# Three products in place of four for the 32 rest channels of a spectral layer

## The chip, the cores and the metric

The kernel runs on one core of a Trainium2 chip. Its time is the device time of one execution in microseconds, the median of several runs. The engines named below are TensorE (PE; its weight loads are PEld), VectorE (DVE), ScalarE (ACT), GpSimd (POOL) and SyncE (SP), which issues most of the DMA transfers.

## The reference

```python
# x: [2, 1, 4096, 640]; w1, w2: [2 (re, im), 4 blocks, 160, 160]; b1, b2: [2, 4, 160]
Xf = rfft2(x, axes=(1, 2))                    # 2049 frequencies
zr, zi = real and imaginary part of Xf.reshape(B, H, Wf, 4, 160)
hr = relu(einsum(zr, w1[0]) - einsum(zi, w1[1]) + b1[0])
hi = relu(einsum(zi, w1[0]) + einsum(zr, w1[1]) + b1[1])
or_ = einsum(hr, w2[0]) - einsum(hi, w2[1]) + b2[0]
oi_ = einsum(hi, w2[0]) + einsum(hr, w2[1]) + b2[1]
a = irfft2(softshrink(or_) + 1j * softshrink(oi_))      # threshold 0.01
b = (gelu(x @ w_gate) * (x @ w_up)) @ w_down            # 640 -> 1728 -> 640
g = sigmoid((x * gate_w).sum(-1))
out = g * a + (1 - g) * b
```

All is fp32, and the kernel reaches that accuracy by splitting operands into a high and a low part (`split`: ScalarE makes the high part in L290, VectorE the low part in L293), so one real product costs three matmuls.

## The kernel before

Three stages follow each other. In the first (0 to about 1315 us) TensorE works on the gate and up projections of the feed-forward part, with the forward Fourier transform's first pass and the preparation of the spectral weights among it. The second is the spectral stage (about 1317 to 1715 us). The third is the down projection with the second pass of the inverse transform.

The change lies in the second. The frequencies are cut into 16 chunks of 256 (one, chunk (0,0), has 258 and is called wide). Each chunk takes four *steps*, one for each block `n` of 160 channels; `steps` lists all 64, and one Python loop over `i` writes the instructions of step `i`, so that order of emission is the order on each engine. For each `i` it writes, in this order: the events of the step (loads; `rest` for the next chunk in the step of block 1), `main_z` of step `i + 1`, `mlp1` of step `i` (layer 1), `mlp2` of step `i - 1` (layer 2), and after every second step the first pass of the inverse transform, `inv1`. Each engine executes its own list in order and waits at semaphores for the others.

A block's 160 channels don't fit 128 partitions. `main_z` transforms the first 128 of them: four L1001 products into one PSUM bank, whose content is split into `z` (high and low; 512 columns hold real and imaginary part). It also makes their sum: ScalarE copies the imaginary part (`zt`, L1013), VectorE adds the real part (L1016), and a split gives `zs`. That split is not written at once: `fwd2` returns it as a function, which `mlp1` calls as `sums()` behind its VectorE additions L1111. The 32 *rest* channels of all four blocks, 128 together, are transformed once per chunk by `rest`, which writes their split `zz` to DRAM (`zld`) so that `zl_load` can bring them back block by block with other partitions.

Layer 1 uses three real products for the 128 main channels: `pk` with the weights times `zs`, and a `group` for each of `hr` and `hi` with `z`, to which `pk` is added (ScalarE copies `pk` to `kc` in L1104, VectorE adds in L1111, then ScalarE and VectorE make `h` in L1064 and L1065). The rest channels enter the two groups by four real products, in two matmuls for each group: `zl1` has 128 rows, `zl2` 66 rows with two rows of ones for the bias. `last` (L1087 to L1089) gives the 32 rest *outputs* into bank `pl`; its last reader is VectorE's L1118, which adds the bias `b1r`. PSUM has eight banks, handed out in turn by `bank()`: a product that takes a bank waits for the last reader of the bank's former content.

The calls that the edit replaces are these:

```python
def rest(b, c):
    z = zmid(b, c, [P, 2, 2, width(b, c)], F32R, name="zz")
    fwd2(b, c, 4 * P, [z[:, h] for h in range(2)])
    ...
at(4 * ch - 3 - lead[1], 1, rest, b, c)
at(4 * ch - 2 - lead[2], 1, zl_load, b, c)
```

Of the kernel before, what the change touches and what calls it, by code (L numbers as in the profile page):

```python
# [43 lines left out]
def _tables():  # L44
# [97 lines left out]
    sgn = np.zeros((P, 4))  # L142
# [3 lines left out]
    sgn[:, 3] = 1 - (p // 2) % 2  # L146
# [21 lines left out]
def _layouts(a):  # L168

    A = lambda n: np.asarray(a[n])  # L170
    c = np.ascontiguousarray
# [41 lines left out]
    def long1(w):
        m, r = w[..., :P], w[..., P:]
        return np.concatenate([m[0], m[1], r[0], r[1]], axis=-1)
# [19 lines left out]
def spectral_mix_kernel(ctx: ExitStack, tc: tile.TileContext, a):  # L235
# [39 lines left out]
    zld = [[dram.tile([P, 4 * CW], F32, name=f"zl_{b}{c}") for c in range(NCH)] for b in range(2)]  # L275
# [580 lines left out]
    def prep(l, pb):  # L856
# [5 lines left out]
        def loads():  # L862
            o["m"] = [small([P, 480], name="raw") for q in range(2)]
            for q in range(2):
                ld(o["m"][q], a[nm + "m"][:, ns[q]])
# [4 lines left out]
        def wide_high(q):  # L870
            m = o["m"][q]
            if l == 1:
# [5 lines left out]
                high(w[:, P:384], m[:, 224:])  # L878
# [5 lines left out]
        def wide_low(q):  # L884
# [4 lines left out]
            if l == 1:  # L889
# [4 lines left out]
                low(w[:, LOW1 + P:], m[:, 224:], w[:, P:384])  # L894
# [4 lines left out]
        def st1():  # L899
            rl, rs = o["l"], o["s"]  # L900
            for m in o["m"] if l == 1 else ():
                nc.vector.tensor_add(m[:, :P], m[:, :P], m[:, 224:352])
                nc.vector.tensor_sub(m[:, 352:], m[:, 352:], m[:, 224:352])
            sg = sgn[:, l - 1:l]
            for cs in ((slice(0, BS),) if l == 2 else (slice(0, P), slice(256, 288))):
                nc.vector.tensor_scalar(rl[:, :, cs], rl[:, :, cs], sg, None, op0=OP.mult)
                nc.vector.tensor_scalar(rs[:64, :, cs], rs[:64, :, cs], sg[:64], None, op0=OP.mult)
            if l == 2:
                nc.vector.tensor_scalar(rs[64:66], rs[64:66], LAM, None, op0=OP.add)
# [6 lines left out]
        def st3():  # L916
            wide_low(1)
            t = o["t"] = big([P, 2, 2, 320], F32R, name="wl")
# [3 lines left out]
            nc.gpsimd.memset(t[64:, :, 1, 0 if l == 2 else 64:].bitcast(F32), 0.0)  # L922
# [3 lines left out]
        def st4():  # L926
            t, bf = o["t"], o["b"].bitcast(F32)
            hi, lo = (t[:, :, 0], t[:, :, 1]) if l == 2 else (t[:, :, 0], t[:, :, 1, 64:])
            n = 320 if l == 2 else 256
            nc.vector.tensor_sub(lo[:64], o["s"][:64, :, :n], bf[:64, :, :n])  # L930
            nc.vector.scalar_tensor_tensor(lo[64:66], bf[64:66, :, :n], sgn[64:66, 2:3], o["s"][64:66, :, :n],
                                           op0=OP.mult, op1=OP.add)
# [22 lines left out]
    zl2, hl1, hl2, HW, WT = [], [], [], {}, []  # L955
# [9 lines left out]
    def ones():  # L965
        zl2.append(mid([P, NBLK, CH], F32R, name="zl2"))
        nc.gpsimd.memset(zl2[-1][64:].bitcast(F32), 0.0)
        nc.gpsimd.memset(zl2[-1][64:66].bitcast(F32), 1.0)

# [57 lines left out]
    def rest(b, c):  # L1027

        z = zmid(b, c, [P, 2, 2, width(b, c)], F32R, name="zz")
        fwd2(b, c, 4 * P, [z[:, h] for h in range(2)])  # L1030
        d = zld[b][c]
        if wide(b, c):
            st(d, z.rearrange("p h r f -> p (h r f)").bitcast(F32))
        else:
            st(dr(d, 0, [[4 * CW, P], [CW, 4], [1, CH]]), z[:, :, :, :CH].rearrange("p h r f -> p (h r) f").bitcast(F32))

    def zl_load(b, c):
        F = width(b, c)
# [5 lines left out]
        ld(t[:, :, :F].bitcast(F32), dr(d, 0, [[CW, P], [P * CW, NBLK], [1, F]]))
        for n in range(NBLK):
            ld(t2[:64, n, :F].bitcast(F32), dr(d, n * P * CW, [[4 * CW, 32], [CW, 2], [1, F]]))
# [20 lines left out]
    def mlp1(b, c, n, sums):  # L1067
# [15 lines left out]
        def last(dst):
# [5 lines left out]
            nc.tensor.matmul(dst, wl[:, 256:384], by_two(t1[:, n, :F]), start=False, stop=True, skip_group_check=True)  # L1089
# [12 lines left out]
        mms(pk[:, :F], [(wh, sh[:, :F]), (wh, sl[:, :F]), (wlo, sh[:, :F])])  # L1102
# [682 lines left out]
```

## Time and profile before

| | |
|---|---|
| median of three runs | 2408.78 us (2407.82 to 2409.89) |
| the profiled execution | 2407.91 us |
| its span in the trace | 2406.1 us |
| spectral stage | about 1317 to 1715 us |
| one chunk of four steps in its middle | 24.7 us |
| TensorE clock granted | 1.00 throughout |

The page gives busy time of each engine, the chain of work that ended last, and groups of equal instructions. The waits view adds up, for one engine, how long an instruction had to wait and which instruction ended the wait; its columns are the total, the number of times and the longest. The timeline lists instructions with start, duration, engine, source line, output and inputs, and in brackets the idle time before them with what ended it. The windows view gives the engines' busy time in stretches of the span.

### The profile page before, as it was taken

Reading aid. Unit: us, or ns where it says so; the run is one execution under the profiler, and the core shown is the slowest. Engines: PE = TensorE matmul, PEld = TensorE weight load, DVE = VectorE, ACT = ScalarE, POOL = GpSimd, SP = SyncE. Lnnn points to the kernel's source line nnn. Section 1 sums busy time; section 2 is a strip of 40 time slices with the busy share of each in tenths; the row PEclk is TensorE's granted clock in tenths of the full one; section 3 lists DMA queues with packets and bytes.
Section 4 is the critical chain, followed back from the end, with each engine's and each line's share of the span. In section 5 each row is a group of like instructions: output and inputs, shape, how many; then the busy total and the mean of one; then the engine's idle time right before and its main releaser. Section 6 shows DMA issues by size and latency. Waiting matters only on the chain.

```text
span 2406.1 us, 49143 instructions
## 1 busy us (share of the span) xinstructions
PE 2397.7 (100%) x18047; PEld 2391.9 (99%) x18047; DVE 1969.7 (82%) x4150; ACT 1464.5 (61%) x3332; POOL 143.0 (6%) x213
## 2 busy tenths in 40 slices
PE   9999999999999999999999999999999999999999
PEld 9999999999999999999999999999999999999999
DVE  8777779777778888888857888888898888888887
ACT  5544456665566666666645788888755555555554
POOL 0111110000000000000001111111000000000000
PEclk9999999999999999999999999999999999999999
DMA  5666666777776777868766454557955544455543
GB/s 213 246 232 235 229 229 231 257 257 252 254 258 228 242 262 239 287 228 268 250 207 230 130 169 152 163 167 234 339 163 165 165 151 152 145 164 165 163 147 98
DMA packets 319093, 503.08 MB, mean 209 GB/s; under 512 B 24444, under 2 KB 196348, under 8 KB 318852
## 3 DMA queue, kind: packets, MB, share of 16 engines
q1 hardware_dynamic: 298788, 446.65, 55.5%
q0 software_dynamic: 20064, 53.29, 6.2%
q8 instruction: 142, 2.33, 0.4%
q14 instruction: 99, 0.81, 0.1%
HBM read 308.74 MB, written 191.11 MB: 208 GB/s over the span
## 4 chain that ended last, share of the span: by engine, by line
PE 91%; issue 5%; DVE 2%; DMA 1%; ACT 1%; SPq 0%; POOL 0%; POOLq 0%; DVEq 0%; ACTq 0%
PE bank L578 70%; PE bank L312 13%; PE bank L1001 3%; PE bank L709 2%; PE bank L832 1%; DMA f<-in_f_dram 1%; PE bank L1087 1%; PE bank L1088 1%; DMA xraw<-in_xT_dram 0%; DVE w L293 0%; PE bank L1089 0%; DVE xo L293 0%; DVE hs L1111 0%; DVE xd L489 0%; ACT m L1148 0%
## 5 line engine op out<-in xcount | busy, mean ns | idle before, releaser
L578 PE MATMUL bank<-xo,w 128*128 128x320 f32 (+1 forms) x9000 | 1250.4, 297 | 0.7 <-ACT p L605 0.7
L578 PEld LDWEIGHTS bank<-xo,w 128*128 128x128 f32 x9000 | 1220.0, 189 | 1.8 <-ACT p L605 1.1
L578 PE MATMUL bank<-wx,ho 128*128 128x320 f32 x4608 | 631.8, 299 | 1.3 <-DVE ho L293 1.1
L578 PEld LDWEIGHTS bank<-wx,ho 128*128 128x128 f32 x4608 | 627.7, 189 | 1.8 <-DVE ho L293 1.4
L293 DVE TENSOR_TENSOR ho<-hraw,ho 128x640 fp32r<-128x640 f32 (+3 forms) x384 | 194.1, 539 | 24.7 <-ACT ho L290 22.7
L605 ACT ACTIVATE u<-bank 128x320 f32<-128x320 f32 (+1 forms) x250 | 107.4, 430 | 138.1 <-PE bank L578 134.2
L290 ACT ACTIVATE ho<-hraw 128x640 fp32r<-128x640 f32 x320 | 168.9, 571 | 34.5 <-PE bank L578 31.3
L655 DVE TENSOR_TENSOR u<-bank,u 128x320 f32<-128x320 f32 (+1 forms) x165 | 79.9, 485 | 82.7 <-ACT u L605 81.8
L293 DVE TENSOR_TENSOR xs<-xr,xs 64x640 fp32r<-64x640 f32 x128 | 104.9, 820 | 46.6 <-ACT xs L290 43.3
L834 DVE TENSOR_TENSOR as<-bank,as 64x320 f32<-64x320 f32 x256 | 113.8, 483 | 25.9 <-ACT as L833 24.1
L293 DVE TENSOR_TENSOR xo<-xraw,xo 128x640 fp32r<-128x640 f32 (+1 forms) x155 | 125.0, 806 | 8.1 <-ACT xo L290 6.1
L312 PE MATMUL bank<-wm,h 128*128 128x320 f32 (+1 forms) x792 | 129.3, 299 | 0.0
L605 ACT ACTIVATE p<-bank 128x320 f32<-128x320 f32 (+1 forms) x125 | 54.1, 432 | 119.3 <-PE bank L578 61.9
L833 ACT ACTIVATE as<-bank 64x320 f32<-64x320 f32 x256 | 96.6, 426 | 32.3 <-PE bank L832 29.3
L290 ACT ACTIVATE xo<-xraw 128x640 fp32r<-128x640 f32 (+1 forms) x155 | 111.7, 721 | 5.4 <-DMA xraw<-in_xT_dram 3.6
L1405 ACT ACTIVATE bank<-bank 128x320 f32<-128x320 f32 x31 | 13.1, 422 | 166.4 <-PE bank L578 166.4
L312 PEld LDWEIGHTS bank<-wm,h 128*128 128x128 f32 (+1 forms) x792 | 111.8, 186 | 1.1
L1399 DVE SCALAR_TENSOR_TENSOR uu<-bank,gs,uu 128x320 f32<-128x320 f32 x193 | 102.5, 545 | 8.4 <-PE bank L578 4.9
L1371 DVE SCALAR_TENSOR_TENSOR uu<-bank,gs,uu 128x320 f32<-128x320 f32 x120 | 57.9, 545 | 49.2 <-ACT uu L1370 47.1
L290 ACT ACTIVATE xs<-xr 64x640 fp32r<-64x640 f32 x128 | 93.4, 730 | 2.1 <-DMA xr<-in_x_dram 0.3
L606 ACT ACTIVATE h<-bank 128x320 f32<-128x320 f32 (+1 forms) x165 | 71.1, 431 | 35.8 <-PE bank L578 32.8
L605 ACT ACTIVATE pb<-bank 128x320 f32<-128x320 f32 x80 | 35.0, 437 | 88.8 <-PE bank L578 88.6
(184 smaller groups left out, 3520.7 us busy)
## 6 DMA issues: line engine op xcount, KB each, us to landing
xo<-xD SPq DMA_DIRECT2D x96, 640.0 KB
xraw<-in_xT_dram SPq DMA_DIRECT2D x158, 320.0 KB
hD<-h SPq DMA_DIRECT2D x128, 320.0 KB
hraw<-hD SPq DMA_DIRECT2D x128, 320.0 KB
xD<-xo POOLq DMA_DIRECT2D x48, 640.0 KB, 4.4
sc<-scr SPq DMA_DIRECT2D x65, 320.0 KB
xr<-in_x_dram SPq DMA_DIRECT2D x64, 320.0 KB
scr<-as SPq DMA_DIRECT2D x64, 320.0 KB
```

Source lines behind the costliest of these rows:

```text
L290: nc.scalar.activation(dst, src, AF.Copy, scale=scale)
L293: eng.tensor_sub(dst, src, hi.bitcast(F32))
L312: nc.tensor.matmul(dst, l, by_two(r), start=i == 0, stop=i == len(ops) - 1)
L578: nc.tensor.matmul(dst, l, by_two(r), start=first and i == 0, stop=i == len(ops) - 1, skip_group_check=True)
L605: copy = lambda d, s_: nc.scalar.activation(d, s_, AF.Copy)
L606: gelu = lambda d, s_: nc.scalar.activation(d, s_, AF.Gelu_apprx_tanh)
L655: nc.vector.tensor_add(u4, C, u4)
L833: nc.scalar.activation(stg[hi, cs], pa[lo, :320], AF.Copy)
L834: nc.vector.tensor_add(stg[hi, cs], pa[hi, :320], stg[hi, cs])
L1001: nc.tensor.matmul(pz.rearrange("p (r e k f) -> p k r e f", r=2, e=2, k=4)[:, kp], SC[b, c, kp][:, o:o + P], ft.rearrange("p (r e f) -> p ...
L1371: nc.vector.scalar_tensor_tensor(uu[n2][:, cs], po[:, :320], gs[b][:, k, n2:n2 + 1], uu[n2][:, cs], op0=OP.mult, op1=OP.add)
L1399: nc.vector.scalar_tensor_tensor(dst, x, g, dst, op0=OP.mult, op1=OP.add)
```

## The change

The rest channels of layer 1 are now also done by three real products. Their contribution to `pk` is one matmul with stacked operands of 96 rows (high, low and high part of the sum against high, high and low weights); each group gets one matmul of 98 rows in place of two, the two extra rows being ones for the bias. So a step has 17 matmuls of 256 columns in layer 1 where it had 18.

For this `rest` also forms the sum of real and imaginary part and its split (`fwd2(..., zs)()`, called at once), and the scratch row in DRAM has six parts in place of four. It is written by four stores in place of one. `zl_load` runs once per step, two steps ahead, into one buffer of four parts, by five loads: three of 32 rows for the stacked operands and two of 64 rows for `last`; GpSimd sets the two rows of ones each time. Before it ran once per chunk, with one load of 128 rows and four of 64. The preparation of the layer-1 weights is reworked to fit; it lies in the first stage.

```diff
 def rest(b, c):
-    z = zmid(b, c, [P, 2, 2, width(b, c)], F32R, name="zz")
-    fwd2(b, c, 4 * P, [z[:, h] for h in range(2)])
+    F = width(b, c)
+    z = zmid(b, c, [P, 2, 2, F], F32R, name="zz")
+    zs = [tiny([P, F], F32R, name="zs") for h in range(2)]
+    fwd2(b, c, 4 * P, [z[:, h] for h in range(2)], zs)()
     d = zld[b][c]
-    if wide(b, c):
-        st(d, z.rearrange("p h r f -> p (h r f)").bitcast(F32))
-    else:
-        st(dr(d, 0, [[4 * CW, P], [CW, 4], [1, CH]]), z[:, :, :, :CH].rearrange("p h r f -> p (h r) f").bitcast(F32))
+    for h in range(2):
+        st(dr(d, 3 * CW * h, [[6 * CW, P], [CW, 2], [1, F]]), z[:, h].bitcast(F32))
+        st(dr(d, 3 * CW * h + 2 * CW, [[6 * CW, P], [1, F]]), zs[h].bitcast(F32))

-def zl_load(b, c):
+def zl_load(b, c, n):
     F = width(b, c)
-    t = ZL1[b, c] = zmid(b, c, [P, NBLK, F], F32R, name="zl1")
-    t2 = ZL2[b, c] = big([66, NBLK, CW], F32R, name="zl2") if F == CW else zl2[chunks.index((b, c)) % 2]
...
-    ld(t[:, :, :F].bitcast(F32), dr(d, 0, [[CW, P], [P * CW, NBLK], [1, F]]))
-    for n in range(NBLK):
-        ld(t2[:64, n, :F].bitcast(F32), dr(d, n * P * CW, [[4 * CW, 32], [CW, 2], [1, F]]))
+    t = ZL[b, c, n] = big([P, 4, F], F32R, name="zl")
+    nc.gpsimd.memset(t[96:98, :2].bitcast(F32), 1.0)
+    d, o = zld[b][c], 32 * n * 6 * CW
+    for k, h in enumerate((0, 1, 0)):
+        ld(t[32 * k:32 * k + 32, :3].bitcast(F32), dr(d, o + 3 * CW * h, [[6 * CW, 32], [CW, 3], [1, F]]))
+    for h in range(2):
+        ld(t[64 * h:64 * h + 64, 3].bitcast(F32), dr(d, o + 3 * CW * h, [[6 * CW, 32], [CW, 2], [1, F]]))

     mms(dst, [(wh, z[0][:, r]), (wh, z[1][:, r]), (wlo, z[0][:, r]),
-              (wl[:, P * m:P * m + P], t1[:, n, :F]), (wl[:t2.shape[0], 384 + P * m:512 + P * m], t2[:, n, :F])])
+              (wl[:98, P + P * m:2 * P + P * m], t[:98, r])])
...
-mms(pk[:, :F], [(wh, sh[:, :F]), (wh, sl[:, :F]), (wlo, sh[:, :F])])
+mms(pk[:, :F], [(wh, sh[:, :F]), (wh, sl[:, :F]), (wlo, sh[:, :F]), (wl[:96, :P], t[:96, 2])])
...
-    at(4 * ch - 2 - lead[2], 1, zl_load, b, c)
+for s in range(2, S):
+    at(s - 2, 1, zl_load, *steps[s])
```

In the file after the change the lines of this part lie 14 to 17 further down (L1013 is L1030, L1104 is L1118, L1118 is L1132).

Three places of the order on the engines. The first is ScalarE in the step of block 1 of a chunk in the middle of the stage. Before, with `zz` of `rest`, then `z` and `zt` of `main_z`, and `zs` of `sums()`:

```order
L290 ACTIVATE ys<-y 128x640 x2
L290 ACTIVATE zz<-bank 128x512
L290 ACTIVATE z<-bank 128x512
L1013 ACTIVATE zt<-bank 128x256
L1104 ACTIVATE kc<-bank 128x256
L290 ACTIVATE zs<-zt 128x256
L1064 ACTIVATE h<-hs 128x512
```

and after:

```order
L292 ACTIVATE zz<-bank 128x512
L1030 ACTIVATE zt<-bank 128x256
L292 ACTIVATE zs<-zt 128x256
L292 ACTIVATE z<-bank 128x512
L1030 ACTIVATE zt<-bank 128x256
L1118 ACTIVATE kc<-bank 128x256
L292 ACTIVATE zs<-zt 128x256
L1081 ACTIVATE h<-hs 128x512
```

The first `zt` and the first `zs` are the new ones, of `rest`; they stand between `zz` and `z`, and the new `zs` waits for VectorE's addition.

VectorE at the same place, before:

```order
L293 TENSOR_TENSOR zz<-bank,zz 128x512
L293 TENSOR_TENSOR z<-bank,z 128x512
L1016 TENSOR_TENSOR zt<-bank,zt 128x256
L1111 TENSOR_TENSOR hs<-bank,kc 128x256 x2
L293 TENSOR_TENSOR zs<-zt,zs 128x256
L1065 SCALAR_TENSOR_TENSOR h<-hs,h 128x512
L1118 SCALAR_TENSOR_TENSOR hs<-bank,b1r,hs 64x256
```

and after:

```order
L295 TENSOR_TENSOR zz<-bank,zz 128x512
L1033 TENSOR_TENSOR zt<-bank,zt 128x256
L295 TENSOR_TENSOR zs<-zt,zs 128x256
L295 TENSOR_TENSOR z<-bank,z 128x512
L1033 TENSOR_TENSOR zt<-bank,zt 128x256
L1125 TENSOR_TENSOR hs<-bank,kc 128x256 x2
L295 TENSOR_TENSOR zs<-zt,zs 128x256
L1082 SCALAR_TENSOR_TENSOR h<-hs,h 128x512
L1132 SCALAR_TENSOR_TENSOR hs<-bank,b1r,hs 64x256
```

The addition `zt` and the low part `zs` of `rest` now stand ahead of `z`, and the low part waits for ScalarE's high part.

The third is SyncE's queue over one chunk (`sc` are the inputs of the transform, `scr` the output of `inv1`, `zl_79` and `zl_77` scratch rows in DRAM). Before:

```order
L270 DMA zl_79<-zz 512x1x256
L270 DMA scr_0_70<-is 16x16x320 x2
L1044 DMA zl_19657<-zl_79 128x4x256
L1046 DMA zl_17094<-zl_79 64x1x256 x4
L989 DMA sc<-scr_1_69 128x640 x4
L270 DMA scr_0_70<-is 16x16x320 x2
```

and after:

```order
L272 DMA zl_77<-zz 128x2x256
L272 DMA zl_77<-zs 128x256
L272 DMA zl_77<-zz 128x2x256
L272 DMA zl_77<-zs 128x256
L272 DMA scr_0_70<-is 16x16x320 x2
L1061 DMA zl<-zl_77 32x3x256 x3
L1063 DMA zl<-zl_77 64x1x256 x2
L1061 DMA zl<-zl_77 32x3x256 x3
L1063 DMA zl<-zl_77 64x1x256 x2
L1006 DMA sc<-scr_0_68 128x640 x4
L272 DMA scr_0_70<-is 16x16x320 x2
```

One store has become four, and ten loads instead of five stand ahead of the `sc` loads; ten more follow behind the second `scr` pair.

More of the change, by code (lines that the diff above doesn't have):

```diff
@@ L140, in _tables @@
     v = v.reshape(19, 16, 4, 2, P).transpose(1, 3, 2, 0, 4).reshape(P, 19, P)
-    sgn = np.zeros((P, 4))
+    sgn = np.zeros((P, 5))
     sgn[:, 0] = 1 - 2 * (p % 2)
@@ L145, in _tables @@
     sgn[:, 2] = -(p % 2)
-    sgn[:, 3] = 1 - (p // 2) % 2
+    sgn[:, 3] = 1 - p // 64
+    sgn[64:, 4] = -1.0 * (p[64:] != 96)
     f = lambda a: np.ascontiguousarray(a.astype(np.float32))
@@ L208, in wide1, with thrice @@
         return np.concatenate([m[1], r[1], r[0], r[1], m[0], m[1]], axis=-1)
+    def thrice(w):
+        return np.concatenate([w[0], w[1], w[1]], axis=-1)
     def wide2(w):
         return np.concatenate([w[1], w[0], w[1]], axis=-1)
[L213 to L215 removed]
     def long2(w):
@@ L223, in _layouts @@
     tr = lambda w: c(w.transpose(1, 0, 2))
-    o["w1m"], o["w2m"] = tr(wide1(w1[:, :, :P])), tr(wide2(w2[:, :, :P]))
-    o["w1l"] = c(rows(w1, long1, [(z, i) for i in i32 for h in range(2) for z in range(2)]))
+    turn = rows(w1[..., P:], long2, [(z, i) for h in range(2) for i in i32 for z in range(2)])
+    o["w1m"], o["w2m"] = c(np.concatenate([tr(wide1(w1[:, :, :P])), turn], axis=-1)), tr(wide2(w2[:, :, :P]))
     o["w2l"] = c(rows(w2, long2, [(z, i) for h in range(2) for z in range(2) for i in i32]))
-    o["w1s"] = c(np.concatenate([rows(w1, long1, [(z, i) for i in i32 for z in range(2)]),
-                                 tr(long1(b1)).repeat(2, 0)]))
+    m1 = np.concatenate([tr(thrice(w1[:, :, P:, :P]))] * 3)
+    b1m = b1[..., :P]
+    o["w1s"] = c(np.concatenate([m1, tr(np.concatenate([b1m[0], b1m[0], b1m[1]], axis=-1)).repeat(2, 0)]))
+    o["b1r"] = c(np.concatenate([b1[0, :, 0, P:], b1[1, :, 0, P:]], axis=-1).T)
     o["w2s"] = c(np.concatenate([rows(w2, long2, [(z, i) for z in range(2) for i in i32]),
@@ L274, in spectral_mix_kernel @@
     scr2 = [dram.tile([16, P, 2, D], F32, name=f"scr2_{b}") for b in range(2)]
-    zld = [[dram.tile([P, 4 * CW], F32, name=f"zl_{b}{c}") for c in range(NCH)] for b in range(2)]
+    zld = [[dram.tile([P, 6 * CW], F32, name=f"zl_{b}{c}") for c in range(NCH)] for b in range(2)]
     xD = [dram.tile([P, 4, 4 * half_of(t)], F32, name=f"xD_{t}") for t in range(KEYS)]
@@ L862, in loads @@
         def loads():
-            o["m"] = [small([P, 480], name="raw") for q in range(2)]
+            n = 544 if l == 1 else 480
+            o["m"] = [small([P, n], name="raw") for q in range(2)]
             for q in range(2):
                 ld(o["m"][q], a[nm + "m"][:, ns[q]])
+            if l == 1:
+                o["s"] = [small([98, 384], name="rs") for q in range(2)]
+                for q in range(2):
+                    ld(o["s"][q], a["w1s"][:, ns[q]])
+                return
             o["l"], o["s"] = small([P, 2, 320], name="rl"), small([66, 2, 320], name="rs")
@@ L877, in wide_high @@
                 high(w[:, 512:576], m[:, BS:BS + 64])
-                high(w[:, P:384], m[:, 224:])
+                high(w[:, P:384], m[:, 224:480])
                 return
@@ L893, in wide_low @@
                 low(w[:, 576:640], m[:, BS:BS + 64], w[:, 512:576])
-                low(w[:, LOW1 + P:], m[:, 224:], w[:, P:384])
+                low(w[:, LOW1 + P:], m[:, 224:480], w[:, P:384])
                 return
@@ L899, in st1 @@
         def st1():
-            rl, rs = o["l"], o["s"]
[L901 to L909, printed above, removed]
+            sg = sgn[:, l - 1:l]
+            if l == 1:
+                for m, r in zip(o["m"], o["s"]):
+                    nc.vector.tensor_add(m[:, :P], m[:, :P], m[:, 224:352])
+                    nc.vector.tensor_sub(m[:, 352:480], m[:, 352:480], m[:, 224:352])
+                    nc.vector.tensor_scalar(m[:, 480:512], m[:, 480:512], sg, None, op0=OP.mult)
+                    nc.vector.scalar_tensor_tensor(r[:96, P:2 * P], r[:96, P:2 * P], -1.0, r[:96, :P], op0=OP.mult,
+                                                   op1=OP.subtract)
+                    nc.vector.tensor_sub(r[:96, 2 * P:], r[:96, 2 * P:], r[:96, :P])
+                return
+            rl, rs = o["l"], o["s"]
+            nc.vector.tensor_scalar(rl[:, :, :BS], rl[:, :, :BS], sg, None, op0=OP.mult)
+            nc.vector.tensor_scalar(rs[:64, :, :BS], rs[:64, :, :BS], sg[:64], None, op0=OP.mult)
+            nc.vector.tensor_scalar(rs[64:66], rs[64:66], LAM, None, op0=OP.add)
         def st2():
@@ L917, in st3 @@
             wide_low(1)
+            if l == 1:
+                t = o["t"] = big([P, 2, 512], F32R, name="wl")
+                for q in range(2):
+                    high(t[:98, q, :384], o["s"][q])
+                    high(t[:, q, 384:448], o["m"][q][:, 480:])
+                    dl[ns[q]] = t[:, q]
+                return
             t = o["t"] = big([P, 2, 2, 320], F32R, name="wl")
@@ L921, in st3 @@
             high(t[:, :, 0], o["l"])
-            nc.gpsimd.memset(t[64:, :, 1, 0 if l == 2 else 64:].bitcast(F32), 0.0)
+            nc.gpsimd.memset(t[64:, :, 1].bitcast(F32), 0.0)
             for q in range(2):
@@ L926, in st4 @@
         def st4():
[L927 to L932, printed above, removed]
-            if l == 1:
-                r = o["l"][:, :, 256:]
-                nc.vector.tensor_sub(r, r, hi[:, :, 256:].bitcast(F32))
-                nc.vector.tensor_scalar(t[:, :, 1, :64], r, sgn[:, 3:4], None, op0=OP.mult)
+            t = o["t"]
+            if l == 1:
+                for q in range(2):
+                    r, x = o["m"][q][:, 480:], t[64:98, q, :384]
+                    nc.vector.scalar_tensor_tensor(x, x.bitcast(F32), sgn[64:98, 4:5], o["s"][q][64:98], op0=OP.mult,
+                                                   op1=OP.add)
+                    nc.vector.tensor_sub(r, r, t[:, q, 384:448].bitcast(F32))
+                    nc.vector.tensor_scalar(t[:, q, 448:], r, sgn[:, 3:4], None, op0=OP.mult)
+                return
+            bf = o["b"].bitcast(F32)
+            lo = t[:, :, 1]
+            nc.vector.tensor_sub(lo[:64], o["s"][:64], bf[:64])
+            nc.vector.scalar_tensor_tensor(lo[64:66], bf[64:66], sgn[64:66, 2:3], o["s"][64:66], op0=OP.mult, op1=OP.add)
         return [loads, st1, st2, st3, st4]
@@ L953, in two @@
         return [t[:, h] for h in range(2)]
-    zl2, hl1, hl2, HW, WT = [], [], [], {}, []
+    hl1, hl2, HW, WT = [], [], {}, []
     def part_of(b, c, k):
@@ L963, in part_of @@
         return WT[0][:, k]
[L965 to L968, printed above, removed]
     def ones_h():
@@ L1088, in last @@
                 nc.tensor.matmul(dst, w[:, k:k + P], by_two(z[1][:, r, :F]), start=False, stop=False, skip_group_check=True)
-            nc.tensor.matmul(dst, wl[:, 256:384], by_two(t1[:, n, :F]), start=False, stop=True, skip_group_check=True)
+            nc.tensor.matmul(dst, wl[:, 384:], by_two(t[:, 3]), start=False, stop=True, skip_group_check=True)
         h = two(b, c, "h")
@@ L1489, in spectral_mix_kernel @@
     at(last, 0, rest, *chunks[0])
-    at(last, 2, ones)
-    at(last, 4, ones)
-    at(last, 2, zl_load, *chunks[0])
+    at(last, 2, zl_load, *chunks[0], 0)
+    at(last, 4, zl_load, *chunks[0], 1)
     first_z = []
@@ L1525, in spectral_mix_kernel @@
     at(1, 0, ld, fny, a["f2"][:, 2 * P:])
-    at(1, 0, ld, b1r, dr(a["w1s"], 64 * NBLK * 320 + 2 * P, [[1, 64], [320, NBLK]]))
+    at(1, 0, ld, b1r, a["b1r"])
     slots = {}
@@ L1658, in spectral_mix_kernel @@
         b, c = chunks[ch]
-        lead = (3, 2, 2) if ch == 2 * NCH - 1 else (0, 0, 0)
+        lead = (3, 2) if ch == 2 * NCH - 1 else (0, 0)
         if ch > 1:
```

12 lines of the change are left out of this document (4 added, 8 removed).

## The prediction

> **What bounds the kernel now.** The page comes first: its span and its row of engine totals.
> ```profile
> span 2406.1 us, 49143 instructions
> PE 2397.7 (100%) x18047; PEld 2391.9 (99%) x18047; DVE 1969.7 (82%) x4150; ACT 1464.5 (61%) x3332; POOL 143.0 (6%) x213
> ```
> Read alone, this says that TensorE is the bound everywhere and that each removed product is gained. But the edit lies in the spectral stage only, and the total mixes three stages. The windows view gives the stage's middle and, in its second row, one chunk in it (columns: PE, PEld, DVE, ACT, POOL busy with counts; TensorE clock; DMA share; GB/s).
> ```profile
> 1374.00:1705.00 331.00, 330.45 (x2677) 328.92 (x2677) 286.28 (x630) 271.11 (x655) 41.71 (x28) 1.00 0.58 183
> 1424.60:1449.30 24.70, 24.70 (x202) 24.61 (x201) 21.50 (x47) 20.24 (x50) 3.13 (x2) 1.00 0.52 160
> ```
> A chunk is four steps and lasts 24.7 us. VectorE is idle for 3.2 us of it, ScalarE for 4.5. The question is what that idle time waits for, so I read the waits of the two engines over 1400 to 1640 us, about ten chunks (ScalarE's rows first).
> ```profile
> ACT zs L290 <- DVE zt L1016: 32.0, 38, 0.9
> ACT h L1064 <- DVE hs L1111: 9.0, 39, 0.3
> ...
> DVE h L1065 <- ACT h L1064: 14.5, 39, 0.4
> DVE ys L293 <- ACT ys L290: 4.9, 20, 0.3
> DVE z L293 <- PE bank L312: 3.3, 6, 0.6
> ```
> This is the finding on which all rests. ScalarE waits for VectorE, never for TensorE; VectorE waits for ScalarE, and the one PE row (3.3 us in ten chunks) is a wait that names several engines. So the two run an in-order loop, each waiting for the other and neither for matmuls: they are behind TensorE, and their idle time is the loop's own latency, not reserve. Where does TensorE meet this loop? The timeline shows the start of two steps: the last L1001 product of an inverse-free stretch and the first layer-1 product (`zs,wm`) behind it, with VectorE's L1118 and L1149 in the second case.
> ```profile
> 1432.25 1.05 PE L1001 MATMUL bank<-f,sc 128*128 128x128 f32 x8
> 1433.06 0.58 PE L312 MATMUL bank<-zs,wm 128*128 128x256 f32 x3
> ...
> 1444.03 1.05 PE L1001 MATMUL bank<-f,sc 128*128 128x128 f32 x8
> 1444.98 0.60 PE L312 MATMUL bank<-zs,wm 128*128 128x256 f32 x3
> ...
> 1444.46 0.47 DVE L1118 SCALAR_TENSOR_TENSOR hs<-bank,b1r,hs 64x256 f32<-64x256 f32 x1
> ```
> Eight L1001 products start 0.81 us ahead of the next matmul at 1432, but 0.95 at 1444, where L1118 of the step before ends at 1444.46 + 0.47 = 1444.93 and the matmul starts 0.05 later. L1118 is the last reader of the PSUM bank that this matmul takes over. TensorE loses 0.14 us there, too little to show as idle, and it shows that the loop, not the matmuls, sets the pace.
>
> **The change, part by part.** (1) *Matmuls.* Per step two groups lose one product each, `pk` gains one, so 18 products of 256 columns become 17, in 64 steps. The spacing is read off the timeline: five products start between these rows.
> ```profile
> 1452.57 0.28 PE L1087 MATMUL bank<-z,wm 128*128 128x256 f32 x1
> ...
> 1453.13 0.98 PE L312 MATMUL bank<-wm,h 128*128 128x320 f32 x6
> ```
> 0.56 / 5 = 0.112 us; 64 x 0.112 = 7.2 us of TensorE time less. What of it counts depends on (2).
>
> (2) *`rest`, once per chunk.* It now makes the sum of real and imaginary part as well: ScalarE gets a copy (L1013's kind) and a high part, VectorE an addition (L1016's kind) and a low part. They are emitted before the next step's `z`, and each waits for the other engine. The rows of a chunk's second step, where `rest` lies; ScalarE, then VectorE, then TensorE:
> ```profile
> 1452.70 0.58 ACT L290 ACTIVATE zz<-bank 128x512 fp32r<-128x512 f32 x1
> 1453.17 0.59 ACT L290 ACTIVATE z<-bank 128x512 fp32r<-128x512 f32 x1
> 1453.65 0.37 ACT L1013 ACTIVATE zt<-bank 128x256 f32<-128x256 f32 x1
> 1453.91 0.38 ACT L1104 ACTIVATE kc<-bank 128x256 f32<-128x256 f32 x1
> 1455.11 0.42 ACT L290 ACTIVATE zs<-zt 128x256 fp32r<-128x256 f32 x1 [0.82 <-DVE zt L1016]
> ...
> 1453.31 0.69 DVE L293 TENSOR_TENSOR zz<-bank,zz 128x512 fp32r<-128x512 f32 x1 [0.28 <-ACT zz L290]
> 1454.05 0.69 DVE L293 TENSOR_TENSOR z<-bank,z 128x512 fp32r<-128x512 f32 x1
> 1454.66 0.41 DVE L1016 TENSOR_TENSOR zt<-bank,zt 128x256 f32<-128x256 f32 x1
> 1454.99 0.74 DVE L1111 TENSOR_TENSOR hs<-bank,kc 128x256 f32<-128x256 f32 x2
> ...
> 1457.04 0.47 DVE L1118 SCALAR_TENSOR_TENSOR hs<-bank,b1r,hs 64x256 f32<-64x256 f32 x1
> ...
> 1456.93 1.05 PE L1001 MATMUL bank<-f,sc 128*128 128x128 f32 x8
> 1457.74 0.58 PE L312 MATMUL bank<-zs,wm 128*128 128x256 f32 x3
> ```
> I place the new order on these times, with the rows' own distances (a 512-column ScalarE start to the next 0.47, a 256-column one 0.26 to 0.31, of which I take 0.31, hand-over about 0.03, `z` to `zt` on VectorE 0.61). ScalarE: `zz` 1452.70, the new copy 1453.17, done 1453.54. VectorE: `zz` 1453.57 (its wait now covers the copy), the new addition 1454.18, done 1454.59. ScalarE: the new high part 1454.63; only then `z` at 1454.94 (was 1453.17) and `zt` 1455.42, done 1455.79. VectorE: the new low part 1455.08, then `z` at 1455.82 instead of 1454.05. So everything behind, `hs`, `h` and L1118, comes 1.77 us later. If the copy may not overlap `zz`, and `zt` not `z`, it is 1.99. L1118 would end at 1459.28 where it ended at 1457.51, and the `zs,wm` product that wants its bank at 1457.74 had 0.2 us of slack: TensorE stalls about 1.6 us per chunk. The loop meets no other engine on its way round, so the whole 1.77 stays in the period.
>
> The lower bound is bare VectorE time, 0.41 + 0.41 = 0.8 per chunk; the upper is 2.0. I take 1.77, the value placed on the rows of that very step.
>
> (3) *How often.* Sixteen calls. The first lies in the FFN stage among matmuls that don't use its result: 0. The second (start of the stage) falls where loop and TensorE already meet: 1.9 at most. The third falls in the 258-column chunk, where ScalarE does wait for TensorE:
> ```profile
> 1359.62 0.52 ACT L1148 ACTIVATE m<-bank,neg2lam 2x320 f32<-2x320 f32 x1 [0.56 <-PE bank L312]
> ```
> With several such waits there it is absorbed: 0.1. The other 13 pay 1.77 each: 23.0. Sum 25.0 us.
>
> (4) *The removed products* are then worth nothing in the 13 chunks: the work that covers them is the loop, which gets no shorter by them. Only around the 258-column chunk, five steps, could 5 x 0.112 = 0.55 us come back; I leave it out. Without (2) they would be worth at most the few tenths per chunk that TensorE is behind the loop, and then the loop is the bound.
>
> (5) *Loads, stores, memsets.* SyncE issues all of it in order; a chunk of before:
> ```profile
> 1454.03 0.54 SPq L270 DMA_DIRECT2D zl<-zz  x1
> 1459.38 1.21 SPq L270 DMA_DIRECT2D scr<-is  x2
> 1460.69 0.56 SPq L1044 DMA_DIRECT2D zl<-zl  x1
> 1461.30 2.71 SPq L1046 DMA_DIRECT2D zl<-zl  x4
> 1464.06 3.32 SPq L989 DMA_DIRECT2D sc<-scr  x4
> 1471.48 1.24 SPq L270 DMA_DIRECT2D scr<-is  x2
> ```
> The sum is 9.6 us in 24.7. After: 4 stores, 20 loads at 2.71 / 4 = 0.68, the same `sc` and `scr`: 4 x 0.54 + 20 x 0.68 + 3.32 + 2.45 = 21.5 of 26.4 us. It fits, and the idle time of this queue covers it; the `sc` loads now stand behind ten `zl` loads and are those that come late first. Each `zl` load is asked for two steps, some 12 us, before its use. I take 0; if the cover goes, an `sc` that is 1 to 3 us late adds that per chunk. The memset of two rows per step goes to POOL, busy 3.1 of 24.7 us: 0. The other weight preparation lies in the FFN stage, whose TensorE work covers it: 0 (some tenths either way).
>
> [...]
>
> **The rivals.** *1, the other side: TensorE is the bound.* Mechanism: L1118 of the second step still ends before its bank is wanted, because VectorE and ScalarE catch up elsewhere in the chunk. The point that decides: 0.2 us of slack at the `zs,wm` product against the loop's extra latency. For it: PE and PEld near 100%. Against: no wait of ScalarE for TensorE in ten chunks. It gives 64 x 0.112 = 7.2 less: 2401.6.
> *2, the loop takes half of it up.* Only the bare VectorE work, 0.8 per chunk, counts, since ScalarE fills its 0.82 wait with the new high part: 13 x 0.8 + 1 = 11.4, so 2420. Against it: the new high part stands ahead of `z` in order, so that wait isn't where it lands.
> *3, loads come late.* SyncE at 21.5 us per chunk: if the `sc` or `zl` loads miss by 1 us in 13 chunks beyond the stall above, 25 + 13 = 38 more, 2447. For it: 20 short loads in place of 5. Against: the DMA share of 0.52 and queue slack of about 5 us.
> *4, no change.* The extra latency is what the removed products pay: 2408.8. It needs the loop to absorb all but 0.5 per chunk (7.2 / 13).
>
> **How the numbers follow.** The profiled execution took 2407.91 us, the median is 2408.78, so the sum 2407.91 + 25.0 = 2432.9 stands for 2433.8 at the median; I say 2433.5. Chances: forecast (1.5 to 2.0 per chunk) 0.60, rival 2 0.15, rival 3 0.12, rival 4 0.05, rival 1 0.08. Range: from rival 2 (2420, rounded down to 2419) to 2.0 per chunk with 15 paying calls plus 1 (2408.8 + 31 = 2440) and a little of rival 3: 2442. It leaves out rivals 1, 4 and most of 3, about 0.2. Faster by over 0.2% (about 5 us, what a measurement of this kernel can tell): rival 1, 0.08; within 0.2%: rival 4, 0.05; slower: 0.87.
>
> **What the profile after would show.** Right: ScalarE's waits get a second `zs` row of `rest` behind VectorE's addition; VectorE's L1118 of the second step ends about 1.8 us later against the L1001 before it; the `zs,wm` product behind it has a visible PE idle time (about 1.6 us) that names L1118; the chunk lasts 26.4 us where it was 24.7; the chain of waits passes through VectorE and ScalarE once per chunk. Wrong: a chunk of 24.3 us with PE without gaps (rival 1), PE idle that names `zl` or `sc` loads (rival 3), or ScalarE waiting for TensorE in every step, which would mean that the loop has reserve.

## The result, and the profile after

The changed kernel takes 2450.54 us (2450.13 to 2452.71, four runs), the kernel before 2408.77 in the same comparison: a ratio of 1.0176 (95% interval 1.0163 to 1.0189), 41.8 us slower. The direction and the main mechanism were forecast. The size was not: 25 us were forecast, and the time lies outside the range of 2419 to 2442.

The page of the kernel after, span and totals:

```profile
span 2450.9 us, 50023 instructions
PE 2413.5 (98%) x17983; PEld 2394.3 (98%) x17983; DVE 1984.5 (81%) x4191; ACT 1477.0 (60%) x3368; POOL 169.3 (7%) x270
```

TensorE executes 64 products fewer, as meant, and VectorE and ScalarE do only 15 and 13 us more; the span is 44.8 us longer. So this is waiting, not work. The waits of the spectral stage's middle, 1400 to 1640 us (total, times, longest), of TensorE, ScalarE and VectorE:

```profile
PE bank L314 <- DVE hs L1132: 7.9, 17, 0.6
PE bank L314 <- DVE zt L1033: 1.9, 8, 0.3
PE bank L314 <- ACT kc L1118: 1.7, 8, 0.3
...
ACT zs L292 <- DVE zt L1033: 40.6, 45, 1.2
ACT h L1081 <- DVE hs L1125: 8.7, 36, 0.2
...
DVE h L1082 <- ACT h L1081: 13.1, 36, 0.4
DVE z L295 <- ACT zt L1030: 8.4, 18, 0.6
DVE zz L295 <- ACT zt L1030: 5.0, 9, 0.6
DVE zs L295 <- ACT zs L292: 4.9, 9, 0.5
```

Before, TensorE had no wait of its own in this stretch. Now it waits 11.5 us in about nine chunks, most of it for L1132 (L1118 before), the last reader of the bank. The loop of the two other engines has two kinds of wait more, both of `rest`: `zz` for the copy, and the low part `zs` for the high part. One step of block 1 shows it in order of time; ScalarE, VectorE, TensorE:

```profile
1466.45 0.58 ACT L292 ACTIVATE zz<-bank 128x512 fp32r<-128x512 f32 x1
1466.92 0.37 ACT L1030 ACTIVATE zt<-bank 128x256 f32<-128x256 f32 x1
1468.44 0.42 ACT L292 ACTIVATE zs<-zt 128x256 fp32r<-128x256 f32 x1 [1.15 <-DVE zt L1033]
1468.76 0.58 ACT L292 ACTIVATE z<-bank 128x512 fp32r<-128x512 f32 x1
...
1467.33 0.69 DVE L295 TENSOR_TENSOR zz<-bank,zz 128x512 fp32r<-128x512 f32 x1 [0.54 <-ACT zt L1030]
1467.93 0.41 DVE L1033 TENSOR_TENSOR zt<-bank,zt 128x256 f32<-128x256 f32 x1
1468.89 0.43 DVE L295 TENSOR_TENSOR zs<-zt,zs 128x256 fp32r<-128x256 f32 x1 [0.54 <-ACT zs L292]
1469.71 0.69 DVE L295 TENSOR_TENSOR z<-bank,z 128x512 fp32r<-128x512 f32 x1 [0.39 <-ACT zt L1030]
...
1472.70 0.47 DVE L1132 SCALAR_TENSOR_TENSOR hs<-bank,b1r,hs 64x256 f32<-64x256 f32 x1
...
1469.94 0.68 PE L314 MATMUL bank<-ys,i 128*128 128x320 f32 x3 [0.20 <-ACT kc L1118]
1470.88 0.65 PE L314 MATMUL bank<-ys,i 128*128 128x320 f32 x3 [0.26 <-DVE zt L1033]
...
1473.22 0.60 PE L314 MATMUL bank<-zs,wm 128*128 128x256 f32 x3 [0.62 <-DVE hs L1132]
```

From ScalarE's `zz` to VectorE's `z` it is 1469.71 - 1466.45 = 3.26 us; before it was 1454.05 - 1452.70 = 1.35. The loop is 1.91 us longer in this step, between the forecast's 1.77 and 1.99.

The other parts are seen by comparing, step by step, when the first `zs,wm` product of a step starts on TensorE (differences to before, in us, read off the timelines of one profiled execution each; the last row is the difference of the spans, which differs from that of the medians by some 4 us at most). e4 has no column, because its profiled execution was a slow one (3573 us at a granted clock of 0.65):

| place | after | e1 | e2 | e3 | e5 | e6 | e11 | e12 |
|---|---|---|---|---|---|---|---|---|
| step 0 (start of the stage) | 5.6 | 6.6 | -0.1 | -0.2 | 0.4 | 5.6 | 2.5 | 0.6 |
| step 9 | 8.0 | 6.6 | 2.7 | -0.8 | 2.7 | 8.0 | 3.0 | -0.6 |
| step 52 | 28.6 | 11.4 | 22.6 | -0.8 | 23.4 | 28.7 | 9.4 | -7.5 |
| step 62 | 33.4 | 15.2 | 26.3 | -0.4 | 28.6 | 35.9 | 16.3 | -9.6 |
| end | 44.8 | 25.3 | 26.4 | 8.8 | 37.6 | 39.0 | 15.1 | -9.2 |

In after, 5.6 us are lost ahead of the stage, 23.0 from step 0 to 52 (about 1.9 per chunk from step 9 on), and 16.2 from step 52 on, in the *tail*: the last chunks and the change to the third stage. Up to 3.7 of the last can still be `rest`'s, since e2, which changes no load, loses as much from step 52 to 62; at least 12.5 are the tail's own. The first loss is a single place in the feed-forward stage; ScalarE's row, TensorE's row, and the windows view of the time just after (behind POOL's figure stand the granted clock, the DMA engines' busy share and GB/s):

```profile
1288.29 0.44 ACT L607 ACTIVATE u<-bank 128x320 f32<-128x320 f32 x1 [3.88 <-DMA zl<-zs]
...
1288.78 4.66 PE L580 MATMUL bank<-xo,w 128*128 128x320 f32 x20 [3.56 <-ACT u L607]
...
1288.80:1289.40 0.60, 0.60 (x4) 0.60 (x5) 0.57 (x2) 0.29 (x1) 0.00 (x0) 0.92 0.00 0
...
1289.30:1292.70 3.40, 3.40 (x15) 3.40 (x14) 3.27 (x11) 1.40 (x6) 0.63 (x1) 0.50 0.00 0
1292.70:1296.10 3.40, 3.40 (x26) 3.40 (x26) 3.40 (x15) 2.30 (x10) 0.52 (x1) 1.00 0.03 7
```

ScalarE's `u` takes a small buffer that a `zs` of the first `rest` had, and the store that reads it lands late; TensorE stands still for 3.56 us and then runs for 3.4 us at a granted clock of 0.50, which makes most of the other 2 us (by estimate 1.7, half of 3.4). The last part is the tail, where TensorE waits for transfers (waits from 1640 to 1800 us; before there were none for a transfer). With the stall of 2.88 us the granted clock falls too: it is 0.50 from 1746.7 us, 0.5 us before the stall ends, to 1753.5 us; the last row, of the windows view, is from that stretch:

```profile
PE bank L314 <- DMA zl<-zl: 4.1, 2, 2.9
PE bank L580 <- DMA wx<-wdf: 3.4, 3, 2.4
...
PE bank L1018 <- DMA sc<-scr: 1.6, 3, 1.0
...
1747.17 0.55 PE L314 MATMUL bank<-zl,wl 96*128 96x256 f32 x1 [2.88 <-DMA zl<-zl]
...
1747.00:1751.00 4.00, 3.83 (x17) 3.86 (x18) 2.24 (x5) 1.46 (x4) 0.00 (x0) 0.50 0.93 247
```

How this load came late is in the chain of work that ended last (1725 to 1748 us), with two of SyncE's own waits from 1730 to 1748 us in the first rows:

```profile
SPq L1296 <- DMA wx<-wdf: 2.7, 1, 2.7
...
SPq L1278 <- DMA scr<-is: 0.8, 1, 0.8
...
1728.43 10.79 DMA scr<-is
...
1739.28 0.32 SPq L1278
...
1740.59 6.44 DMA zl<-zl
1747.04 0.14 issue
1747.17 0.98 PE bank L314 x3
```

SyncE issues in the order of its list. The last step's `zl` loads stand behind loads for the third stage (`s` in L1296, `wx` in L1278), and these wait for other transfers: `s` 2.7 us for a `wx`, and `wx` until a store of `inv1` (`scr`) has landed, 10.79 us after its issue. Only then are the `zl` loads issued, and one of them takes 6.44 us to land.

### The profile page after: what moved, and what is told of

It is laid out like the page before. It is cut to its first block, busy times and chain, and to the rows that moved or that the text cites. A ratio compares the mean times of both kernels' runs of the same rounds, so it can differ in the third digit from the quotient of the medians.

```text
span 2450.9 us, 50023 instructions
## 1 busy us (share of the span) xinstructions
PE 2413.5 (98%) x17983; PEld 2394.3 (98%) x17983; DVE 1984.5 (81%) x4191; ACT 1477.0 (60%) x3368; POOL 169.3 (7%) x270
## 4 chain that ended last, share of the span: by engine, by line
PE 86%; DMA 4%; DVE 4%; ACT 3%; issue 1%; SPq 1%; DVEq 0%; ACTq 0%
PE bank L580 73%; PE bank L314 7%; PE bank L711 2%; PE bank L834 1%; DMA zl<-zl 1%; PE bank L1018 1%; DMA sc<-scr 1%; DMA scr<-is 1%; DVE hs L1125 1%; ACT h L1081 1%; ACT ys L292 1%; DVE zt L1033 1%; ACT z L292 1%; DVE h L1082 1%; DMA xraw<-in_xT_dram 0%
## 5 line engine op out<-in xcount | busy, mean ns | idle before, releaser
L295 DVE TENSOR_TENSOR ho<-hraw,ho 128x640 fp32r<-128x640 f32 (+3 forms) x384 | 194.4, 541 | 28.7 <-ACT ho L292 26.2
L835 ACT ACTIVATE as<-bank 64x320 f32<-64x320 f32 x256 | 96.6, 426 | 31.7 <-PE bank L834 28.6
```

The lines of the kernel that those rows point to most:

```text
L295: eng.tensor_sub(dst, src, hi.bitcast(F32))
L835: nc.scalar.activation(stg[hi, cs], pa[lo, :320], AF.Copy)
```

## The experiments

The theory: the kernel after is slower because `rest`'s sum stands in the in-order loop of ScalarE and VectorE, plus two separate terms, the buffer and the tail's queue. The rivals are these: the loads and the longer queue cost it all; the added engine work costs it wherever it stands; TensorE is the bound and something hides the gain.

### e1: the split of rest's sum, later

```diff
-    fwd2(b, c, 4 * P, [z[:, h] for h in range(2)], zs)()
+    f = fwd2(b, c, 4 * P, [z[:, h] for h in range(2)], zs)
+    if (b, c) == chunks[0]:
+        f()
+    else:
+        later.append(f)
...  # mlp1
     sums()
+    while later:
+        later.pop()()
     relu_split(h[0], h[1], hs)
```

> After, but the split of rest's sum is written behind the split of the next step's sum (in sums() of the same step) instead of at once; the copy and the addition stay where they are, and so do loads, stores and matmuls. Theory (the in-order loop of ScalarE and VectorE is lengthened by the split that stands ahead of z, about 1.9 us per chunk): on the rows of before, z on VectorE then comes 0.46 us later instead of 1.8, so a chunk lasts about 25.1 us where after has 26.6; 13 x 1.4 = 18 us less than after, about 2432. Rival (the loads of zl and the longer SyncE queue cost the time): no change, 2450. Rival (the ScalarE and VectorE work as such costs it, wherever it stands): no change, 2450.

Measured: 2432.60 us, ratio 1.0100 (1.0086 to 1.0114). The same work, loads and matmuls in another order are worth 18 us. From step 9 to 52 the stage loses 4.8 us where after lost 20.6. Both rivals fall for this part.

### e2: before, with rest's sum and nothing else

```diff
+    zs = [tiny([P, width(b, c)], F32R, name="zs") for h in range(2)]
-    fwd2(b, c, 4 * P, [z[:, h] for h in range(2)])
+    fwd2(b, c, 4 * P, [z[:, h] for h in range(2)], zs)()
```

> Before, with rest also making the sum and its split at once, as after does; the result is not stored or used, matmuls, loads and stores are those of before. Theory (the loop): the same 1.9 us per chunk as after shows, 13 x 1.9 + 2 = about 27 us, 2435, and a chunk of 26.5 us. Rival (loads and queue): 2409. By the bare VectorE work alone (0.8 us per chunk): 2420.

Measured: 2434.52 us, ratio 1.0109 (1.0094 to 1.0125): 26.1 us, all of it between step 0 and the end of the stage, none ahead of it and none in the tail (table). VectorE's row in the step of block 1 shows the same wait as after:

```profile
1463.35 0.42 DVE L293 TENSOR_TENSOR zs<-zt,zs 128x256 fp32r<-128x256 f32 x1 [0.54 <-ACT zs L290]
```

So the sum alone, without one changed load or product, makes the stage's loss (22.7 us from step 0 to 52, 23.0 in after).

### e3: after, without rest's sum

```diff
-    fwd2(b, c, 4 * P, [z[:, h] for h in range(2)], zs)()
+    fwd2(b, c, 4 * P, [z[:, h] for h in range(2)])
...
-        st(dr(d, 3 * CW * h + 2 * CW, [[6 * CW, P], [1, F]]), zs[h].bitcast(F32))
+        st(dr(d, 3 * CW * h + 2 * CW, [[6 * CW, P], [1, F]]), z[:, h, 0].bitcast(F32))
```

> After, but rest makes no sum: its two stores of the sum send the real part instead, so the rest channels' contribution is not the reference's; matmuls, stores and loads in number and size as after. Theory (the loop): the chunk goes back to 24.6 us; what is left over before is what the stores, loads and the last chunks' queue cost, estimated from after's trace (3.8 at one late sc, 1.3 and up to 10 at the end of the stage) at 5 to 15 us: 2414 to 2424. Rival (TensorE is the bound once the loop is short): 2402 plus that remainder. Rival (loads and queue cost all of it): 2450.

Measured: 2417.95 us, ratio 1.0042 (1.0029 to 1.0056). Up to step 62 this kernel is 0.4 us ahead of before; then the tail costs it 9. Waits of TensorE from 1640 to 1900 us:

```profile
PE bank L580 <- DMA wx<-wdf: 3.8, 3, 2.4
PE bank L314 <- DMA zl<-zl: 2.4, 1, 2.4
PE bank L1018 <- DMA sc<-scr: 1.1, 2, 0.7
```

In the steady chunks the 20 loads and 4 stores cost nothing, as forecast; in the tail they do. And with the loop back at its old length, 17 products win no more than 1.3 us at any step of the stage: TensorE isn't the bound.

### e4: before, with 17 products

```diff
-mms(pk[:, :F], [(wh, sh[:, :F]), (wh, sl[:, :F]), (wlo, sh[:, :F])])
+mms(pk[:, :F], [(wh, sh[:, :F]), (wh, sl[:, :F])])
```

> Before, with the third product of pk left out in every step (17 products of 256 columns as in after), so the weights' low part is missing from pk; nothing else changes. Theory (the loop sets the pace of the spectral stage, TensorE has no say in 13 of 16 chunks): 0 to 1.5 us less than before. Rival (TensorE is the bound there): 64 x 0.112 = 7.2 us less.

Measured: 2407.73 us, ratio 0.9998 (0.9989 to 1.0007). 64 products of 0.112 us are taken away and 0.6 us comes of it, less than the measurement can tell from nothing. The rival that TensorE bounds the stage falls.

### e5: another buffer for the first zs

```diff
-zs = [tiny([P, F], F32R, name="zs") for h in range(2)]
+zs = [(mid if (b, c) == chunks[0] else tiny)([P, F], F32R, name="zs") for h in range(2)]
```

> After, but for the first call of rest (in the FFN stage) the two buffers of the sum's split come from the pool of large buffers instead of the one that the FFN's u tiles use too; nothing else changes. Theory (there ScalarE's copy to u waits 3.9 us for the store of zs that still reads the buffer, TensorE stands for 3.6 us and then runs at a granted clock of 0.5 to 0.6 for 4 us): step 0 of the spectral stage starts 5.6 us earlier than in after, 2445. Rival (the delay there comes from the changed weight preparation or the extra VectorE work): 2450.

Measured: 2445.50 us, ratio 1.0153 (1.0139 to 1.0167), 5.0 us less than after; step 0 is 0.4 us late where it was 5.6. TensorE's wait there falls from 3.56 to 0.4 us.

### e6: the tail's zl loads from GpSimd's queue

```diff
 def zl_load(b, c, n):
+    ld = nc.gpsimd.dma_start if (b, c) >= (1, 4) else nc.sync.dma_start
```

> After, but the zl loads of the last four chunks (b = 1, c from 4) are issued from GpSimd's queue instead of SyncE's. Theory (in the last chunks SyncE issues the zl loads, the sc loads and the down projection's weights in order and falls behind, so sc and zl come late): the late sc (3.8 us at step 53), the late zl (1.3 and 2.9) and a good part of the 10 us after step 63 go, 8 to 14 us less than after, 2437 to 2442; the steady chunks stay at 26.6 us. Rival (the data are late for lack of DMA bandwidth, whichever queue issues them): 2450.

Measured: 2443.22 us, ratio 1.0147 (1.0133 to 1.0161): 7.3 us less than after, a little short of the 8 to 14 expected. The late `sc` is gone, which was 3.8 us at step 53. What is left in TensorE's waits (1640 to 1860 us), and on GpSimd, whose own queue now holds a load back:

```profile
PE bank L580 <- DMA wx<-wdf: 2.6, 1, 2.6
PE bank L314 <- DMA zl<-zl: 2.3, 1, 2.3
...
POOL zl L1062 <- DMA zl<-zs: 8.7, 3, 4.2
```

So the place of these loads in SyncE's queue is the cause of about half of the tail's own loss (5.8 us less in the spans, of at least 12.5). The rest stays open: the stores of `zl` still stand on SyncE, and one load is still 2.3 us late. The rival that the data come late for lack of bandwidth isn't ruled out for this rest, since the DMA engines' busy share is 1.02 to 1.03 here from 1720 to 1760 us (before had 0.95 to 1.01 in its tail, 1700 to 1745 us).

### e8: before, the low part ahead of the copy

This and the next but one were attempts to shorten the loop. VectorE's `z` waits for ScalarE's copy `zt` as well as for `z` (the copy ended the wait 4 times, 2.2 us in all, in before from 1400 to 1640 us), so I wrote its instruction ahead of the copy:

```diff
 high(zz[0], pr)
+low(zz[1], pr, zz[0])
 if zs:
     ...
     nc.scalar.activation(t4, pr[:, 1], AF.Copy)
-low(zz[1], pr, zz[0])
```

> Before, with that last edit alone: low part ahead of the copy in fwd2. Theory (the loop sets the pace by 0.2 us per chunk in 13 chunks, then TensorE bounds): 2 to 3 us less, about 2406. Rival (the wait for the copy costs the loop nothing, or TensorE is the bound already): no change, 2408.5.

Measured: 2427.81 us, ratio 1.0083 (1.0069 to 1.0096): 19.3 us slower, a clear miss. ScalarE's wait and one step of it, and VectorE's `z`:

```profile
ACT zt L1014 <- DVE z L293: 30.4, 37, 0.9
...
1463.97 0.59 ACT L290 ACTIVATE z<-bank 128x512 fp32r<-128x512 f32 x1
1465.39 0.38 ACT L1014 ACTIVATE zt<-bank 128x256 f32<-128x256 f32 x1 [0.83 <-DVE z L293]
...
1464.67 0.68 DVE L293 TENSOR_TENSOR z<-bank,z 128x512 fp32r<-128x512 f32 x1
```

The copy now waits for VectorE, 37 times and 30.4 us in all. In before VectorE's `z` starts 0.02 to 0.04 us behind the end of the copy in each of the 39 steps from 1400 to 1640 us; here, in the step shown, the copy starts at 1465.39 us, 0.04 behind the end of `z` (1464.67 + 0.68). So in both kernels the one that is written first reads this bank first, and the other waits for its end; why, no run shows. As evidence on the loop the miss is strong: no work, load or product was added, only one hand-over per step, and from step 9 to 52 the kernel pays 1.4 us per chunk.

### e7: e1, e5, e6 and e8's edit together

> After with the deferred split of the first experiment, the other buffer for the first call, GpSimd's queue for the zl loads of the last four chunks, and one more edit: in fwd2 the low part is written ahead of the copy of the imaginary part, so VectorE's z waits for ScalarE's z alone and not for the copy as well. Theory: the loop gets shorter by some 0.3 us per step than in the first experiment and TensorE with 17 products becomes the bound, so the chunk lasts about 24.1 us; with the two other terms gone the kernel takes 2400 to 2410, about 2404. Rival (the loop keeps the extra 0.5 us per chunk): 2414. Rival (the tail's loads stay late): 2415 and more.

Measured: 2444.25 us, ratio 1.0150 (1.0136 to 1.0164), another miss. Adding up the single runs gives 2450.5 - 17.9 - 5.0 - 7.3 + 19.3 = 2439.6, so e8's edit takes back most of what the other three give; no run has those three without it. ScalarE's largest wait (1400 to 1640 us) is e8's here too, the copy behind VectorE's `z`: 28.0 us.

### e9 and e10: the sum moved behind h

```diff
 # mlp1: the two groups of products stand ahead of pk, and
-sums()
+sums[0]()          # VectorE's addition zt
 relu_split(h[0], h[1], hs)
 ...
 nc.vector.scalar_tensor_tensor(hs, pl[:64, :F], b1r[:, n:n + 1], hs, op0=OP.add, op1=OP.add)
+sums[1]()          # the split of zs
```

> Before, with the sum taken off the loop: in mlp1 the two groups are multiplied ahead of pk, VectorE's addition zt stands behind its two hs additions (there it fills the wait for ScalarE's h), and the split of zs stands behind L1118. No work is added or left out. Theory (the loop sets the pace): each step's loop loses 0.33 us, so TensorE with its 18 products becomes the bound at about 24.45 us per chunk: 2 to 4 us less than before, about 2405.5. Rival (zs now comes too late for the next step's pk): 2409 to 2415.

> The same, with pk's third product left out in every step, so 17 products of 256 columns (the weights' low part is missing from pk). Theory: with the loop out of the way the removed product pays now, up to 0.112 us in each step, 3 to 7 us less than the kernel just above; in the kernel before it paid 0.6. Rival (the loop is still the bound): 0 to 1 us less than the kernel above.

Measured: e9 2410.40 us, ratio 1.0007 (0.9998 to 1.0016); e10 2408.27 us, 1.0000 (0.9991 to 1.0008). The first didn't shorten the loop (ScalarE's and VectorE's largest waits in e9, 1400 to 1640 us):

```profile
ACT h L1066 <- DVE hs L1113: 45.1, 39, 1.2
...
DVE h L1067 <- ACT h L1066: 15.0, 39, 0.4
```

VectorE waits for `h` as long as before (15.0 us against 14.5). Most likely the addition now fills the gap that the low part of `zs` filled, and the low part is paid for elsewhere; no run separates the two. From step 9 to 49 a chunk takes 24.8 us, before's 24.9. The 17 products then win 2.1 us over e9, between the two expectations.

### e11: after, repaired

After with e5, e6, e9's order for both sums, and the last two steps' loads two steps earlier.

> After with the same order (the groups ahead of pk, the additions of the sums behind the hs additions, the splits behind L1118, for rest as for main_z), the other buffer for the first call, GpSimd's queue for the zl loads of the last four chunks, and those of the last two steps two steps earlier. Theory: the loop is about 24.2 us per chunk and TensorE's 17 products 24.0, the FFN term (5.6 us) is gone, the tail keeps 3 to 6 us: 2404 to 2410. Rival (rest's added work still lengthens the loop by 0.5 us per chunk or more): 2415 and more.

Measured: 2422.86 us, ratio 1.0056 (1.0044 to 1.0069): 27.7 us better than after, still slower than before, as the rival had it. It loses 6.4 us from step 9 to 52, and 6.9 more to step 62, where `zl` loads come late (TensorE waits 4.7 us for two of them, 3.7 for one).

### e12: 17 products, and the loop really shorter

e4's edit, and VectorE's addition `zt` left out:

```diff
-if zs:
-    nc.vector.tensor_add(t4, pr[:, 0], t4)
```

> Before with 17 products (pk's third left out, as in the fourth experiment) and without VectorE's addition zt, so zs is the imaginary part alone. The last two but one did not make the loop shorter: VectorE's wait for h stayed at 0.4 us per step, since what filled it had only moved. Here 0.33 us of VectorE time per step really goes from the loop. Theory (loop against TensorE; the removed product pays as soon as the loop is out of the way): the chunk falls from 24.65 us to TensorE's own 24.0, 13 x 0.65 + 1 = 7 to 10 us less than before, 2399 to 2402. Rival (something else holds the chunk at 24.6 us): 2407.5, as in the fourth experiment.

Measured: 2397.69 us, ratio 0.9953 (0.9940 to 0.9967), 11.3 us less than before, a little more than expected. From step 9 to 52 it gains 6.9 us, and ScalarE now waits for matmuls ten times in these ten steady chunks, if only for 0.2 us each (1400 to 1640 us):

```profile
ACT m L1146 <- PE bank L312: 1.9, 10, 0.2
ACT z L290 <- PE bank L1001: 0.9, 2, 0.6
```

Without the addition's 64 instructions in the loop the same 17 products come with a gain that e4 didn't have. But there is no run with the addition left out and 18 products, so it isn't shown how much of the 11.3 us is the products'. By estimate it is 7.2 at most (64 times 0.112), so that at least 4.1 are the shorter loop's.

## Why the prediction was wrong, point by point

*What bounds the kernel: right.* The waits view, in which ScalarE and VectorE name almost only each other, decided against the 99% of the weight loads. Rival 1, TensorE as the bound, would have given 2401.6. The runs do not agree with it: e4 takes the products away and nothing moves, e2 adds to the loop alone and 26.1 us come.

*Part 2, rest: right.* 1.77 to 1.99 us per chunk were placed by hand, and 1.91 measured in the step shown; 25.0 us were forecast for the stage, and e2 has 26.1. The bare VectorE time of rival 2 was not the price. Two details were off. TensorE does not stand 1.6 us at the `zs,wm` product: it stands 0.62 there and 0.20 and 0.26 at two products of `inv1` ahead of it, 1.3 us per chunk in all. And the third call, put at 0.1 because the 258-column chunk would absorb it, costs 0.9 in e2 (whose delay against before goes from 1.8 us at step 4 to 2.7 at step 6).

*Part 4, the removed products: right*, worth 0 to 1 us (e3, e4).

*Part 3, the first call of rest, "0": wrong, 5.0 us* (e5). The first step that failed is "among matmuls that don't use its result". The result isn't used, but the buffer is: the `u` of the feed-forward stage takes it over and waits 3.88 us for a store. The working followed data and never the buffers that the new tiles share.

*Part 5, loads and stores, "0": right in the steady chunks, wrong in the tail, 9.6 us* (e3, as a whole kernel against before). This is the second step that failed: "the idle time of this queue covers it" was worked out for a chunk in the middle, and for a queue that only has to issue. In the last chunks the down projection's loads (`wx`, `s`, `hraw`) share the queue. Around the late `sc` it issues for 21.4 of 26 us (1664 to 1690). At the late last `zl` it isn't full; it stands still behind loads that wait for other transfers. Over the whole tail, 1640 to 1745 us, it issues for 72% of the time, against 68% in the steady chunks, so the sum of its issue times doesn't show the trouble. Rival 3 named late `sc` and `zl`, but priced them in the steady chunks and gave it 0.12; the range reached only "a little" into it. Both failed terms had a place outside the stretch from which the durations were taken.

The sum of the parts, each measured by itself, is 26.1 (e2) + 9.6 (e3) + 5.0 (e5) = 40.7 us of the 41.8. Each part is uncertain by about 3 us, so that the sum comes this close is in part luck.

## What to carry to other kernels

If two engines name almost only each other in the waits view over a long stretch, ask whether their loop is the bound, however full a third one is; here it was, beside a TensorE at 99%. An added instruction can then be placed on their rows by hand, with each hand-over; here that gave 1.77 us where 1.91 was measured. Work that is moved or added must be followed in three further ways that the data flow doesn't show: who takes over its buffer, what else stands in its queue at the stage's edges, and which instructions of two engines wait for each other at one PSUM bank (in e8 37 waits, 30.4 us). A queue is to be read where most kinds of transfer share it, not where the loop is steady, and for what its instructions wait for in order, not only for the time that they take to issue.

## What the runs showed of the hardware

A stall of TensorE cost more than its length here. After standing still for 3.56 us it was granted a clock of 0.92 on average for 0.6 us, then 0.50 for 3.4 us; 3.56 us of waiting became 5.6 us of delay. The stall of 2.88 us behind the last `zl` load came with 0.50 for 6.8 us (1746.7 to 1753.5). The late `sc` in front of step 53 had 0.50 for 3.4 us behind it, though there TensorE waited only 1.6 us in three pieces; the windows before and after, and for comparison one of a steady chunk with its stalls:

```profile
1675.00:1678.40 3.40, 1.91 (x12) 1.31 (x10) 3.00 (x8) 3.16 (x8) 0.00 (x0) 1.00 0.97 327
1678.40:1681.80 3.40, 3.25 (x13) 2.96 (x14) 1.70 (x4) 1.90 (x4) 2.18 (x3) 0.50 1.07 351
...
1469.90:1473.30 3.40, 2.48 (x15) 1.92 (x15) 3.04 (x8) 2.24 (x5) 0.00 (x0) 1.00 0.62 205
```

The granted clock was 0.50 behind 3.4 us in which TensorE was busy for 1.91, and stayed at 1.00 (1473.3 to 1480.0 us) behind 3.4 us in which it was busy for 2.48; what sets it, no run shows. The 3.8 us at step 53 are thus 1.6 us of waiting and, by estimate, 1.7 us of half clock (half of 3.4).
